# Full-width taps in one five-bank PSUM tile, a fixed split with GpSimd, and summed transforms on TensorE

## The chip, the cores and the metric

The kernel runs on one core of a Trainium2 chip. The metric is the device time of one execution in microseconds (us); lower is better. The kernel before takes 3369.24 us (median of three runs, 3368.65 to 3371.1).

## The reference

Three stages follow each other on `x` of 4 batches, 4224 tokens and 192 features.

```
w   = softmax(weight_gen over its 7 taps)         # per token and head, 8 heads of 24 features
y1[s] = sum over k of w[s, head, k] * x[s - 6 + k]  # a causal convolution of 7 taps, weights of its own per token
u   = y1 + real(fft over tokens (fft over features (y1)))
u   = u + relu(layernorm(u) @ w_ch1) @ w_ch2
th  = u @ w_theta
v   = u + w_tok_r @ (u cos th) + w_tok_i @ (u sin th)   # two 4224 x 4224 matrices over tokens
out = v + relu(v @ w_ch)
```

The change lies in the first line of work, the convolution, and in the Fourier transform that follows it.

## The kernel before, in words

The function `prologue` does the convolution and the transform. Tokens stand as 33 columns of 128 (one per partition), and a batch is cut into eight chunks of these columns: the first has five columns, the other seven have four (`SEQ`). With four batches there are 32 chunks, g = 0 to 31. A chunk of four columns and 192 features has 768 elements per partition.

For each chunk the seven taps are divided. GpSimd (`pool_taps`) multiplies the first three taps (four in the last chunk of a batch, `NPOOL`) and adds them up in a tile `pa`. VectorE (`dve_taps`) does the others: each tap is a multiplication and an addition, on two halves of 96 features. The products lie in PSUM tiles `t` of half width, three of them in rotation (`ps_t`); the running sum lies in SBUF (`xn`, named `acc` in the code). One multiplication has its weights from PSUM: ScalarE copies them into one of two PSUM tiles `wbank` (`dve_weights`, L159), always for the chunk after the next one to be computed, so that the copy for chunk g+1 is issued as chunk g begins. At the end the partial sum `pa` is added, the chunk is stored to DRAM (`xs`), and the next chunk begins.

The weights of two chunks are made by one `softmax` on 448 (or 504) elements: maximum, difference, exponential on ScalarE, sum, `1e-9` added, reciprocal, product. Its steps are set between the taps of every even chunk (`SOFT` tells after which).

The transform is a list of small steps in a queue. `rotated(d)` takes two finished chunks: TensorE turns them (L211, L223, L225), multiplies by the feature transform (L237 to L242), and ScalarE copies each result out of PSUM. `spectrum(b)` follows when a batch is complete. It has 14 groups of features: `first` (L274, then a ScalarE copy `A`, L276) and, for each pair of groups, `second` (eight matmuls L282 to L285 into two sums U and V), a ScalarE copy of U (L287), and `join`, four VectorE instructions that form U+V and U-V into `mxt`. One step of the queue is issued after every second piece of a chunk's taps (`step(1)`), eight in a chunk. All three of `first`, `second` and the turns share three PSUM buffers (`ps_f`).

Each engine works through its own instructions strictly in the order in which this code issues them. So a ScalarE copy for the transform that waits for TensorE holds back whatever ScalarE was given later: the exponential of the next softmax, or the copy of the next weights. Weights for the later stages are converted in between as well (`state["weights"]`).

When the last chunk is stored, the last batch's transform is finished beside the first steps of `main_phase`; then the large matmuls over tokens (L893) run to the end.

Of the kernel before, what the change touches and what calls it, by code (L numbers as in the profile page):

```python
# [10 lines left out]
F32 = mybir.dt.float32  # L11
# [5 lines left out]
AF = mybir.ActivationFunctionType  # L17
# [6 lines left out]
P = 128  # L24
# [2 lines left out]

SEQ = ((0, 5), (29, 4), (5, 4), (25, 4), (9, 4), (21, 4), (13, 4), (17, 4))
XO = [sum(n + 6 for _, n in SEQ[:c]) for c in range(9)]
SOFT = (1, 2, 4, 5, 7, 8)  # L30
NPOOL = (3, 3, 3, 3, 3, 3, 3, 4)
TCH = 352
NCH = S // TCH
HCH = NCH // 2
# [18 lines left out]
C2 = 0.0019353071795864769  # L53
PIC = 3.1415925
NWTS = 2 * DFF + 9 * D
NCONST = 588 + 256 + 256 + 3 * 119


def run_all(gen):
# [4 lines left out]
def prologue(tc, I, xs, mx, state):  # L64
# [12 lines left out]
    wp = pool(actx, "pw", 2)  # L77
    gp = pool(actx, "pg", 2)

    ps_w = pool(actx, "psw", 1, space=PSUM)  # L80
    wbank = [ps_w.tile([P, 512], F32, name=f"wbank{i}") for i in range(2)]
    ps_t = pool(actx, "pst", 3, space=PSUM)

    const = cp.tile([P, NCONST], F32, name="const")
    MD = const[:, 0:588].rearrange("p (s c) -> p s c", s=3)
    CS = const[:, 588:844]
    DI = const[:, 844:1100]
    BD = [const[:119, 1100 + 119 * i : 1219 + 119 * i] for i in range(3)]

    xin, wn, xn, taps, wpss = {}, {}, {}, {}, {}  # L90
    queue = state["queue"] = collections.deque()

    def load_x(g):
# [16 lines left out]
    def softmax(d):  # L110
        w, n = wn[d]
        w = w[:, :n]
        m = wbank[1][:, 5 * H * K : 5 * H * K + n]
        wide = m.unsqueeze(2).to_broadcast([P, n, K])
        nc.vector.tensor_reduce(out=m, in_=w, axis=AX.X, op=ALU.max)
        yield
        nc.vector.tensor_tensor(out=w, in0=w, in1=wide, op=ALU.subtract)
        nc.scalar.activation(w, w, AF.Exp)
        yield
        nc.vector.tensor_reduce(out=m, in_=w, axis=AX.X, op=ALU.add)  # L120
        yield
        nc.vector.tensor_scalar(m, m, 1e-9, None, op0=ALU.add)
        yield
        nc.vector.reciprocal(m, m)
        yield
# [16 lines left out]

    def pool_taps(g):
        b, c, n, d, jl = place(g)
        nt = NPOOL[c]
# [8 lines left out]
        taps[g] = (nt, pa)  # L154

    def dve_weights(g):
        b, c, n, d, jl = place(g)
        wps = wbank[g % 2][:, : 5 * H * K].rearrange("p (q k) -> p q k", k=K)
        nc.scalar.copy(wps[:, : n * H], wn[d][0][:, jl * H : (jl + n) * H])  # L159
        return wps  # L160

    def dve_taps(g):
        b, c, n, d, jl = place(g)
        nt, pa = taps.pop(g)
# [4 lines left out]
        halves = [(slice(4 * i, 4 * i + 4), slice(96 * i, 96 * i + 96)) for i in range(2)]  # L169
        ts = [None, None]  # L170
        for k in range(nt, K):
            for i, (hs, _) in enumerate(halves):
                if k == nt:
                    o = hv(xn[d], jl, n, hs)
                else:
                    ts[i] = ps_t.tile([P, 5, 96], F32, tag="tmp", name=f"t{g}{k}{i}")
                    o = hv(ts[i], 0, n, None)
                nc.vector.tensor_tensor(out=o, in0=hv(xin[g], k, n, hs), in1=wv(wps, 0, n, k, hs), op=ALU.mult)
                yield
            if k == K - 1:  # L180
                for i, (_, fs) in enumerate(halves):
                    t = ts[i][:, :n]
                    nc.vector.tensor_tensor(out=t, in0=t, in1=pa[:, :n, fs], op=ALU.add)
                    yield
            if k > nt:
                for i, (_, fs) in enumerate(halves):
                    nc.vector.tensor_tensor(out=acc[:, :, fs], in0=ts[i][:, :n], in1=acc[:, :, fs], op=ALU.add)  # L187
                    yield
        j0 = SEQ[c][0]
        nc.sync.dma_start(out=xs[b // 2][j0 : j0 + n, :, b % 2, :].rearrange("j p d -> p j d"), in_=acc)  # L190

    PQ, MX = {}, {}

# [57 lines left out]
    def spectrum(b):  # L251

        mxt = state["mxt"] = f1.tile([P, NF, D], F32, tag="mxt", name=f"mxt{b}")
        done = []

        def join(gg, ps, u):
            for i in range(2):
                V = ps[:, i, 1].rearrange("p (k e) -> p k e", e=7)
                c = 14 * gg + 7 * i
                n = 6 if c == 91 else 7  # L260
                nc.vector.tensor_tensor(
                    out=mxt[:, :, 95 + c : 95 + c + n], in0=u[:, i, :, :n], in1=V[:, :, :n], op=ALU.add
                )
                n = 5 if c == 91 else 7
                nc.vector.tensor_tensor(
                    out=mxt[:, :, c : c + n], in0=u[:, i, :, :n], in1=V[:, :, :n], op=ALU.subtract
                )

        A = {}

        def first(g):
            ps = ps_f.tile([P, 512], F32, tag="f", name=f"ps1{b}{g}")
            for c in range(2):
                nc.tensor.matmul(ps[:119, c * 256 : c * 256 + 256], PQ[b][:, c, g], CS, start=True, stop=True)  # L274
            a = A[g] = f3.tile([P, 4, P], F32, tag="A", name=f"A{b}{g}")
            nc.scalar.copy(a[:119].rearrange("p s k -> p (s k)"), ps[:119])  # L276

        def second(gg):
# [12 lines left out]
        yield  # L291
        first(1)
        yield
        for gg in range(7):
            if gg < 6:
                first(2 * gg + 2)
                yield
            r = second(gg)
            if gg < 6:
                first(2 * gg + 3)  # L300
            yield
            join(*r)
# [19 lines left out]
    for g in range(8 * B):  # L322
        if g + 2 < 8 * B:
            load_x(g + 2)
        if g % 2 and g // 2 + 2 < 4 * B:
            load_w(g // 2 + 2)
        soft = softmax(g // 2 + 1) if g % 2 == 0 and g // 2 + 1 < 4 * B else iter(())
        if g % 2 and g + 1 < 8 * B:
            pool_taps(g + 1)
        if g + 1 < 8 * B:  # L330
            wpss[g + 1] = dve_weights(g + 1)
        for n, _ in enumerate(dve_taps(g)):
            if n in SOFT:
                next(soft, None)
            if g >= 6 and n % 8 == 3:
                next(state["weights"], None)
            if n % 2:
                step(1)
        if g % 2 == 0 and g + 1 < 8 * B:
            pool_taps(g + 1)  # L340
        if g % 2:
            queue.append(rotated(g // 2))
        if g % 8 == 7:
            queue.append(spectrum(g // 8))
    actx.close()
    state["fft"] = fctx
    state["step"] = step
# [584 lines left out]
def constants():  # L932
# [11 lines left out]
    be = 2 * np.pi * ((8 * np.outer(j, j)) % NJ) / NJ  # L944
    e7 = np.eye(7)
    pad = np.zeros((P - 119, 119))
    bd = [np.concatenate([np.kron(v, e7), pad]) for v in (np.cos(be), np.sin(be), -np.sin(be))]
# [68 lines left out]
```

## Time and profile before

| | |
|---|---|
| runs, median (range) | 3369.24 us (3368.65 to 3371.1) |
| span of the profiled execution | 3368.4 us |
| TensorE matmuls | busy 3227.4 us, 96% |
| VectorE | busy 2376.5 us, 71% |
| ScalarE | busy 2096.9 us, 62% |
| GpSimd | busy 717.7 us, 21% |
| mean granted TensorE clock | 0.984 |

The page gives no other time for the profiled execution than its span, 0.8 us under the median of the runs. A span of 3368 us cut into 40 slices makes slices of 84 us; the prologue fills the first four of them. Shares over the whole span say little on it, so the rows further down are nearly all from the first 325 us.

### The profile page before, as it was taken

What the parts mean: (1) busy time and instruction counts of PE and PEld (TensorE: products, weight loads), DVE (VectorE), ACT (ScalarE), POOL (GpSimd) and SP (SyncE); (2) the same over time, 40 slices, a digit from 0 to 9 for tenths busy, and PEclk for the clock granted to TensorE, in tenths of its full rate; (3) what the DMA queues carried; (4) which work ended last, traced back from release to release, by engine and by line L of the source; (5) the groups of instructions that cost most, each with busy time, mean ns of one, the idle gap of its engine ahead of it and who ended that gap; (6) DMA issues with size and microseconds to landing.
All of it is one profiled execution on the core that took longest, in us unless ns stands there. A gap on an engine that the chain in (4) does not pass through costs nothing.

```text
span 3368.4 us, 54351 instructions
## 1 busy us (share of the span) xinstructions
PE 3227.4 (96%) x20980; PEld 3181.8 (94%) x20980; DVE 2376.5 (71%) x5338; ACT 2096.9 (62%) x3230; POOL 717.7 (21%) x662
## 2 busy tenths in 40 slices
PE   4778789999999999999999999999999999999999
PEld 3667689999999999999999999999999999999999
DVE  8998466676666666666666666676666766667666
ACT  1343456666666666666666666666666666666743
POOL 8987111111111111111111111111111111111133
PEclk8889899999999999999999999999999999999999
DMA  5554123333333333333333333333333333333333
GB/s 192 191 183 147 66 78 106 113 111 106 113 105 113 103 110 113 107 111 112 105 113 109 109 113 107 111 108 110 110 103 113 113 105 113 107 111 113 114 122 120
DMA packets 120243, 388.02 MB, mean 115 GB/s; under 512 B 10160, under 2 KB 64048, under 8 KB 119472
## 3 DMA queue, kind: packets, MB, share of 16 engines
q1 hardware_dynamic: 119696, 383.75, 33.3%
q8 instruction: 164, 2.69, 0.3%
q14 instruction: 95, 0.78, 0.1%
q10 hardware_dynamic: 288, 0.81, 0.1%
HBM read 351.88 MB, written 32.64 MB: 114 GB/s over the span
## 4 chain that ended last, share of the span: by engine, by line
PE 85%; ACT 2%; DVE 1%; POOL 0%; issue 0%; DMA 0%; ACTq 0%; POOLq 0%; DVEq 0%
PE y L893 66%; PE ch L620 4%; PE fy L832 2%; PE ch L621 2%; PE psh L598 1%; PE psh L594 1%; PE psh L597 1%; PE psh L595 1%; PE psh L596 1%; PE pst L684 1%; PE pst L672 1%; PE psu L570 1%; PE psx L650 0%; ACT cq L371 0%; ACT cq L372 0%; DVE f L380 0%
## 5 line engine op out<-in xcount | busy, mean ns | idle before, releaser
L893 PE MATMUL y<-ws,z 128*128 128x352 f32 x14256 | 2470.4, 324 | 8.4 <-DVE acc L490 3.5
L893 PEld LDWEIGHTS y<-ws,z 128*128 128x128 f32 x14256 | 2267.1, 188 | 11.4 <-DVE acc L490 4.6
L488 DVE TENSOR_TENSOR acc<-y,acc 128x352 f32<-128x352 f32 (+1 forms) x1158 | 597.2, 516 | 111.1 <-PE y L893 111.0
L387 ACT CAST ws<-f 128x704 fp32r<-128x704 f32 x396 | 309.7, 782 | 389.1 <-DVE f L380 343.3
L374 DVE SCALAR_TENSOR_TENSOR cq<-cx,cq 128x176 int32<-128x176 int32 x396 | 135.8, 343 | 470.0 <-ACT cq L372 469.6
L371 ACT ACTIVATE cq<-cq,bounds 128x704 uint8<-128x704 uint8 x396 | 348.4, 880 | 162.5 <-DVE cq L368 156.1
L726 POOL TENSOR_TENSOR r<-r,x 128x256 f32<-128x256 f32 (+1 forms) x264 | 191.8, 759 | 1156.8 <-ACT r L719 1156.8
L389 DVE TENSOR_TENSOR ws<-f,ws 128x704 fp32r<-128x704 f32 x396 | 358.0, 904 | 57.9 <-ACT ws L387 57.9
L378 ACT ACTIVATE f<-cq 128x704 int32<-128x704 int8 x396 | 312.8, 790 | 138.1 <-DVE cq L374 138.0
L380 DVE SCALAR_TENSOR_TENSOR f<-raw,f 128x704 int32<-128x704 int32 x396 | 355.9, 899 | 32.2 <-ACT f L378 31.9
L372 ACT ACTIVATE cq<-cq,bounds 128x704 uint8<-128x704 uint8 x396 | 349.3, 882 | 12.9
L366 ACT COPY cx<-raw 128x704 uint8<-128x704 uint8 x396 | 327.3, 826 | 3.1 <-DMA raw<-in_W 3.1
L607 DVE SCALAR_TENSOR_TENSOR g<-psh,g 128x256 fp32r<-128x256 f32 x384 | 162.2, 422 | 209.6 <-ACT g L606 209.6
L553 POOL TENSOR_SCALAR rs<-mv 128x2 f32<-128x2 f32 x66 | 12.6, 192 | 1185.6 <-DVE mv L552 1185.6
L620 PE MATMUL ch<-w2s,g 128*128 128x384 f32 x768 | 241.2, 350 | 1.9 <-ACT g L606 1.9
L621 PE MATMUL ch<-w2s,g 128*128 128x192 f32 x768 | 193.7, 252 | 0.1
L737 POOL TENSOR_TENSOR z<-r,z 128x768 fp32r<-128x768 f32 x66 | 122.0, 1848 | 135.6 <-ACT z L732 135.6
L621 PEld LDWEIGHTS ch<-w2s,g 128*128 128x128 f32 x768 | 145.9, 190 | 2.2 <-DVE g L607 2.0
L606 ACT ACTIVATE g<-psh 128x256 fp32r<-128x256 f32 x384 | 142.7, 372 | 8.1 <-PE ch L621 6.5
L620 PEld LDWEIGHTS ch<-w2s,g 128*128 128x128 f32 x768 | 144.6, 188 | 3.0 <-ACT g L606 2.7
L211 PE MATMUL psT<-const,xn 128*128 128x128 f32 x264 | 47.3, 339 | 92.9 <-DVE xn L187 81.1
L211 PEld LDWEIGHTS psT<-const,xn 128*128 128x128 f32 x264 | 41.8, 242 | 97.6 <-issue 54.6
(159 smaller groups left out, 3896.3 us busy)
## 6 DMA issues: line engine op xcount, KB each, us to landing
raw<-in_W SPq DMA_DIRECT2D x396, 703.6 KB
xin<-in_xa SPq DMA_DIRECT2D x28, 960.0 KB
out<-fo SPq DMA_DIRECT2D x24, 528.0 KB
mx<-mxd SPq DMA_DIRECT2D x65, 192.0 KB
xs<-xn SPq DMA_DIRECT2D x28, 384.0 KB
mxd<-mxt SPq DMA_DIRECT2D x4, 1632.0 KB
xin<-in_xa SPq DMA_DIRECT2D x4, 1056.0 KB
w<-in_wg SPq DMA_DIRECT2D x12, 224.0 KB
```

Of the source, the lines that this page charges most:

```text
L366: nc.scalar.copy(x.bitcast(U8), tops)
L371: nc.scalar.activation(q8, q8, AF.Relu, bias=bounds[:, 0:1], scale=-1.0)
L372: nc.scalar.activation(q8, q8, AF.Relu, bias=bounds[:, 1:2], scale=-8.0)
L378: nc.scalar.activation(ti, q.bitcast(I8), AF.Copy, scale=2.0**24)
L380: nc.vector.scalar_tensor_tensor(ti, words, 5, ti, op0=ALU.logical_shift_right, op1=ALU.bitwise_or)
L387: nc.scalar.copy(h, t)
L389: (eng or nc.vector).tensor_tensor(out=l(), in0=t, in1=h.bitcast(F32), op=ALU.subtract)
L488: nc.vector.tensor_tensor(out=d, in0=v, in1=d, op=ALU.add)
L620: nc.tensor.matmul(ch[:, i, 0 : 2 * D], g[:, 0, t], w, start=ft == 0, stop=False)
L621: nc.tensor.matmul(ch[:, i, D : 2 * D], g[:, 1, t], w[:, :D], start=False, stop=ft == 5)
L726: nc.gpsimd.tensor_tensor(out=o[:, ri], in0=o[:, ri], in1=x[:, :, d], op=ALU.mult)
L893: nc.tensor.matmul(ps[:, 0], zz[hl], s[:, hw, ri], start=q + n == 0, stop=q == parts_n - 1 and n == 2)
```

## The change

Four things are altered in `prologue`, and a table of constants grows by three blocks.

1. The two `wbank` tiles and the three `t` tiles are replaced by one PSUM tile `banks` of five banks (2560 elements per partition). It holds two full-width product areas `prod`, two weight areas `wts`, and the softmax's small row `m`. A tap is now one multiplication and one addition on all 192 features. A chunk's final addition (with its store) is put off until the next chunk's first multiplication has been issued (`ends`).
2. GpSimd takes three taps of every chunk, VectorE four.
3. In the softmax, `1e-9` is added by ScalarE; its steps come after the pieces 0 to 5 of a chunk, which now has eight.
4. For the first three batches TensorE forms both sums of the spectrum itself: `direct` runs eight matmuls of 238 columns for a pair of groups where `second` ran eight of 119, and `place_both` copies both results to `mxt` by ScalarE. `join` and the copy of U are left to the last batch.

```diff
-SOFT = (1, 2, 4, 5, 7, 8)
-NPOOL = (3, 3, 3, 3, 3, 3, 3, 4)
+SOFT = (0, 1, 2, 3, 4, 5)
+NPOOL = 3
...
-    wbank = [ps_w.tile([P, 512], F32, name=f"wbank{i}") for i in range(2)]
-    ps_t = pool(actx, "pst", 3, space=PSUM)
+    TW, WW = 5 * D, 5 * H * K
+    banks = pool(actx, "pst", 1, space=PSUM).tile([P, 2560], F32, name="banks")
+    prod = [banks[:, i * TW : (i + 1) * TW].rearrange("p (j d) -> p j d", d=D) for i in range(2)]
+    wts = [banks[:, 2 * TW + i * WW : 2 * TW + (i + 1) * WW] for i in range(2)]
+    mbase = 2 * (TW + WW)
...
-        nc.vector.tensor_scalar(m, m, 1e-9, None, op0=ALU.add)
+        nc.scalar.activation(m, m, AF.Identity, bias=eps[:, 0:1])
...
-        wps = wbank[g % 2][:, : 5 * H * K].rearrange("p (q k) -> p q k", k=K)
+        wps = wts[g % 2].rearrange("p (q k) -> p q k", k=K)
...
-        for k in range(nt, K):
-            for i, (hs, _) in enumerate(halves):
...
+        mult(sums, 3)
+        yield
+        if ends:
+            ends.pop()()
+            yield
+        mult(hv(prod[0], 0, n, None), 4)
+        yield
+        mult(hv(prod[1], 0, n, None), 5)
+        yield
+        add(acc, t0, acc)
+        yield
+        mult(hv(prod[0], 0, n, None), 6)
+        yield
+        add(acc, t1, acc)
+        yield
+        add(t0, t0, taps.pop(g)[:, :n])
+        yield
...
+        def direct(gg):
+            ps = ps_f.tile([P, 2, 2, 119], F32, tag="f", name=f"ps2{b}{gg}")
+            for i in range(2):
+                a = A.pop(2 * gg + i)[:119]
+                for q, (s, w) in enumerate(BOTH):
+                    nc.tensor.matmul(
+                        ps[:, i].rearrange("p s c -> p (s c)"), a[:, s], w, start=q == 0, stop=q == len(BOTH) - 1
+                    )
+            return gg, ps, None
...
-            r = second(gg)
+            r = (direct if b < 3 else second)(gg)
...
-            join(*r)
+            (place_both if b < 3 else join)(*r)
...
-            if n % 2:
-                step(1)
+            step(1)
```

On VectorE, chunk 7 (an odd one, without softmax) begins like this before. `t` are the half-width products, `wbank` the weights in PSUM, `pa` GpSimd's partial sum.

```order
L178 TENSOR_TENSOR xn_481<-xin_442,wbank_118 128x4x96 [waits DMAHW1_49]
L178 TENSOR_TENSOR xn_481<-xin_442,wbank_118 128x4x96
L178 TENSOR_TENSOR t_584<-xin_442,wbank_118 128x384
L178 TENSOR_TENSOR t_586<-xin_442,wbank_118 128x384 [waits DVE_49]
L187 TENSOR_TENSOR xn_481<-t_584,xn_481 128x4x96 [waits DVE_49]
L187 TENSOR_TENSOR xn_481<-t_586,xn_481 128x4x96 [waits DVE_49]
L178 TENSOR_TENSOR t_590<-xin_442,wbank_118 128x384
L178 TENSOR_TENSOR t_592<-xin_442,wbank_118 128x384 [waits DVE_49]
```

The two halves alternate, so a wait of VectorE on itself names an instruction two or more places ahead. Now the same chunk, whole:

```order
L180 TENSOR_TENSOR banks<-banks,pa_372 128x768 [waits DVE_49,Pool_49]
L177 TENSOR_TENSOR xn_393<-xin_368,banks 128x768 [waits DMAHW0_49,Activation_49]
L180 TENSOR_TENSOR xn_393<-banks,xn_393 128x768
L177 TENSOR_TENSOR banks<-xin_368,banks 128x768 [waits DVE_49] x2
L180 TENSOR_TENSOR xn_393<-banks,xn_393 128x768 [waits DVE_49]
L177 TENSOR_TENSOR banks<-xin_368,banks 128x768 [waits DVE_49]
L180 TENSOR_TENSOR xn_393<-banks,xn_393 128x768 [waits DVE_49]
L180 TENSOR_TENSOR banks<-banks,pa_456 128x768 [waits DVE_49,Pool_49]
```

The first row ends chunk 6. The first multiplication of chunk 7 now waits for ScalarE as well; by the values in the built program it waits for the weight copy of chunk 8. Six of the seven instructions behind it wait for VectorE, each for the instruction directly ahead of it.

On ScalarE, in the middle of the first spectrum, before: A are the copies behind `first`, U those behind `second`, L159 copies the weights of chunk 11, and L118 is the exponential of chunk 10's softmax.

```order
L276 COPY A_769<-ps_766 119x512 [waits PE_49]
L276 COPY A_785<-ps_782 119x512 [waits PE_49]
L287 COPY U_798<-ps_789 128x238 [waits DVE_49,PE_49]
L276 COPY A_803<-ps_800 119x512 [waits PE_49,Activation_49]
L159 COPY wbank_118<-w_571 128x224 [waits DVE_49]
L276 COPY A_822<-ps_819 119x512 [waits PE_49,Activation_49]
L118 ACTIVATE w_705<-w_705 128x448 [waits DMAHW6_49,DVE_49,Pool_49]
```

Now, at the same copy (L165 for the weights, L312 for `place_both`, L128 for the `1e-9`):

```order
L295 COPY A_630<-ps_627 119x512 [waits PE_49]
L312 COPY mxt_551<-ps_618 128x17x14 x2
L295 COPY A_640<-ps_637 119x512 [waits PE_49,Activation_49]
L295 COPY A_655<-ps_652 119x512 [waits PE_49,Activation_49]
L165 COPY banks<-w_466 128x224 [waits DVE_49]
L312 COPY mxt_551<-ps_643 128x17x14 x2
L124 ACTIVATE w_573<-w_573 128x448 [waits DMAHW5_49,DVE_49,Pool_49]
L413 ACTIVATE fw_669<-cqw_497 128x512
L295 COPY A_674<-ps_671 119x512 [waits PE_49,Activation_49]
L295 COPY A_690<-ps_687 119x512 [waits PE_49,Activation_49]
L128 ACTIVATE banks<-banks,eps 128x64 [waits DVE_49,Activation_49]
```

The weight copy stands behind the same copy A of the eighth `first`, in both. What it waits for has moved: by the wait's value, before it is the last multiplication of chunk 9 that reads its own `wbank`; now it is the very last addition of chunk 9, the instruction directly ahead of chunk 10's first multiplication on VectorE.

## Rows read from the trace of the kernel before

**Rows 1.** Windows: busy us of each engine, then granted TensorE clock, DMA share, GB/s.

```profile
280.00:320.00 40.00, 30.77 (x214) 28.06 (x212) 40.00 (x94) 15.42 (x39) 35.87 (x22) 0.91 0.49 165
```

**Rows 2.** Timeline at the last chunk's end: start us, us, engine, line, instruction, [idle before].

```profile
323.25 1.00 DVE L187 TENSOR_TENSOR xn<-t,xn 128x384 f32<-128x384 f32 x2
...
324.40 2.05 PE L211 MATMUL psT<-const,xn 128*128 128x128 f32 x8 [4.25 <-DVE nhalf L463]
```

**Rows 3.** Timeline of the DMA queue: the stores of chunks 7 and 23.

```profile
83.45 0.38 SPq L190 DMA_DIRECT2D xs<-xn  x1
...
245.83 0.38 SPq L190 DMA_DIRECT2D xs<-xn  x1
```

**Rows 4.** Groups by form, VectorE, 0 to 320 us: busy us, mean ns | idle before.

```profile
L178 DVE TENSOR_TENSOR t<-xin,wbank 128x384 f32<-128x384 f32 x158 | 80.9, 549 | 0.0
...
L178 DVE TENSOR_TENSOR t<-xin,wbank 128x480 f32<-128x480 f32 x24 | 15.0, 653 | 0.0
L261 DVE TENSOR_TENSOR mxt<-U,ps 128x119 f32<-128x119 f32 x39 | 10.5, 268 | 2.7 <-ACT U L287 2.7
```

**Rows 5.** VectorE timeline: the starts of chunks 3, 4 and 5.

```profile
40.40 1.01 DVE L178 TENSOR_TENSOR xn<-xin,wbank 128x384 f32<-128x384 f32 x2
...
47.83 1.01 DVE L178 TENSOR_TENSOR xn<-xin,wbank 128x384 f32<-128x384 f32 x2
...
57.97 1.01 DVE L178 TENSOR_TENSOR xn<-xin,wbank 128x384 f32<-128x384 f32 x2
```

**Rows 6.** VectorE timeline: the first softmax, where each instruction waits for the one ahead.

```profile
5.45 0.69 DVE L115 TENSOR_REDUCE wbank<-w 128x72 f32<-128x504 f32 x1 [4.57 <-DMA w<-in_wg]
6.17 0.68 DVE L117 TENSOR_TENSOR w<-w,wbank 128x504 f32<-128x504 f32 x1
7.54 0.69 DVE L120 TENSOR_REDUCE wbank<-w 128x72 f32<-128x504 f32 x1 [0.69 <-ACT w L118]
...
10.32 1.22 DVE L178 TENSOR_TENSOR xn<-xin,wbank 128x480 f32<-128x480 f32 x2 [0.46 <-ACT wbank L159]
```

**Rows 7.** Groups by form, ScalarE, 0 to 320 us.

```profile
L276 ACT COPY A<-ps 119x512 f32<-119x512 f32 x42 | 24.2, 585 | 15.3 <-PE ps L274 15.2
...
L159 ACT COPY wbank<-w 128x224 f32<-128x224 f32 x28 | 10.0, 356 | 50.0 <-DVE t L178 50.0
L287 ACT COPY U<-ps 128x238 f32<-128x238 f32 x21 | 7.5, 355 | 17.8 <-PE ps L285 14.9 <-DVE mxt L265 1.6 <-ACT w1s L387 1.0
...
L230 ACT COPY st<-psS 128x128 f32<-128x128 f32 x4 | 1.0, 261 | 0.0
```

**Rows 8.** TensorE timeline: a batch's last turn and its spectrum; two records make one matmul.

```profile
83.57 2.04 PE L211 MATMUL psT<-const,xn 128*128 128x128 f32 x8 [6.39 <-DVE xn L187]
...
92.64 2.85 PE L274 MATMUL ps<-const,PQ 128*119 128x256 f32 x12 [0.65 <-ACT PQ L245]
...
95.54 0.39 PE L283 MATMUL ps<-const,A 119*128 119x119 f32 x2
95.77 0.39 PE L284 MATMUL ps<-const,A 119*128 119x119 f32 x2
...
97.11 1.89 PE L274 MATMUL ps<-const,PQ 128*119 128x256 f32 x8
98.87 0.48 PE L282 MATMUL ps<-const,A 119*128 119x119 f32 x2
...
120.21 1.06 PE L211 MATMUL psT<-const,xn 128*128 128x128 f32 x8
```

**Rows 9.** Windows as in rows 1: that turn, and that spectrum.

```profile
83.60:88.20 4.60, 4.60 (x28) 3.88 (x28) 4.60 (x9) 1.95 (x4) 4.52 (x3) 0.59 0.84 276
92.60:120.20 27.60, 25.49 (x168) 22.47 (x169) 27.18 (x68) 13.66 (x28) 24.72 (x16) 1.00 0.40 131
```

**Rows 10.** GpSimd timeline: the starts of chunks 2 and 3.

```profile
28.32 1.54 POOL L149 TENSOR_TENSOR pa<-xin,w 128x768 f32<-128x768 f32 x1
...
36.61 1.54 POOL L149 TENSOR_TENSOR pa<-xin,w 128x768 f32<-128x768 f32 x1
```

More of the change, by code (lines that the diff above doesn't have):

```diff
@@ L55 @@
 NWTS = 2 * DFF + 9 * D
-NCONST = 588 + 256 + 256 + 3 * 119
+NCONST = 588 + 256 + 256 + 6 * 119
 def run_all(gen):
@@ L87, in prologue @@
     DI = const[:, 844:1100]
-    BD = [const[:119, 1100 + 119 * i : 1219 + 119 * i] for i in range(3)]
-    xin, wn, xn, taps, wpss = {}, {}, {}, {}, {}
+    bd = lambda i, n: const[:119, 1100 + 119 * i : 1100 + 119 * (i + n)]
+    BD = [bd(0, 1), bd(3, 1), bd(4, 1)]
+    BOTH = ((0, bd(0, 2)), (1, bd(4, 2)), (3, bd(1, 2)), (2, bd(3, 2)))
+    eps = cp.tile([P, 1], F32, name="eps")
+    nc.vector.memset(eps, 1e-9)
+    xin, wn, xn, taps, wpss, ends = {}, {}, {}, {}, {}, []
     queue = state["queue"] = collections.deque()
@@ L112, in softmax @@
         w = w[:, :n]
-        m = wbank[1][:, 5 * H * K : 5 * H * K + n]
+        m = banks[:, mbase : mbase + n]
         wide = m.unsqueeze(2).to_broadcast([P, n, K])
@@ L144, in pool_taps @@
         b, c, n, d, jl = place(g)
-        nt = NPOOL[c]
+        nt = NPOOL
         pa = gp.tile([P, 5, D], F32, tag="pa", name=f"pa{g}")
@@ L153, in pool_taps @@
                 nc.gpsimd.tensor_tensor(out=pa[:, :n], in0=pa[:, :n], in1=t[:, :n], op=ALU.add)
-        taps[g] = (nt, pa)
+        taps[g] = pa
     def dve_weights(g):
         b, c, n, d, jl = place(g)
-        wps = wbank[g % 2][:, : 5 * H * K].rearrange("p (q k) -> p q k", k=K)
+        wps = wts[g % 2].rearrange("p (q k) -> p q k", k=K)
         nc.scalar.copy(wps[:, : n * H], wn[d][0][:, jl * H : (jl + n) * H])
@@ L163, in dve_taps @@
         b, c, n, d, jl = place(g)
-        nt, pa = taps.pop(g)
         wps = wpss.pop(g)
@@ L168, in dve_taps, with mult, add, end @@
         acc = xn[d][:, jl : jl + n]
-        halves = [(slice(4 * i, 4 * i + 4), slice(96 * i, 96 * i + 96)) for i in range(2)]
-        ts = [None, None]
-        for k in range(nt, K):
-            for i, (hs, _) in enumerate(halves):
[L173 to L190, printed above, removed]
+        sums, (t0, t1) = hv(xn[d], jl, n, None), (t[:, :n] for t in prod)
+        def mult(o, k):
+            nc.vector.tensor_tensor(out=o, in0=hv(xin[g], k, n, None), in1=wv(wps, 0, n, k), op=ALU.mult)
+        def add(o, x, y):
+            nc.vector.tensor_tensor(out=o, in0=x, in1=y, op=ALU.add)
+        mult(sums, 3)
[15 more added lines that the diff above has]
+        yield
+        def end():
+            add(acc, t0, acc)
+            j0 = SEQ[c][0]
+            nc.sync.dma_start(out=xs[b // 2][j0 : j0 + n, :, b % 2, :].rearrange("j p d -> p j d"), in_=acc)
+            if g % 2:
+                queue.append(rotated(d))
+            if c == 7:
+                queue.append(spectrum(b))
+        ends.append(end)
     PQ, MX = {}, {}
@@ L276, in first, with place_both @@
             nc.scalar.copy(a[:119].rearrange("p s k -> p (s k)"), ps[:119])
+        def direct(gg):
[7 more added lines that the diff above has]
+            return gg, ps, None
+        def place_both(gg, ps, _):
+            for s, o in enumerate((95, 0)):
+                v = ps[:, :, s].rearrange("p i (k e) -> p k i e", e=7)
+                m = mxt[:, :, o + 14 * gg : o + 14 * gg + (14, 14 - s - 1)[gg == 6]]
+                if gg < 6:
+                    nc.scalar.copy(m.rearrange("p k (i e) -> p k i e", e=7), v)
+                else:
+                    nc.scalar.copy(m[:, :, :7], v[:, :, 0])
+                    nc.scalar.copy(m[:, :, 7:], v[:, :, 1, : 6 - s])
         def second(gg):
@@ L334, in prologue @@
                 next(soft, None)
-            if g >= 6 and n % 8 == 3:
+            if g >= 6 and n % 4 == 1:
                 next(state["weights"], None)
-            if n % 2:
-                step(1)
+            step(1)
         if g % 2 == 0 and g + 1 < 8 * B:
             pool_taps(g + 1)
[L341 to L344, printed above, removed]
+    ends.pop()()
     actx.close()
@@ L946, in constants @@
     pad = np.zeros((P - 119, 119))
-    bd = [np.concatenate([np.kron(v, e7), pad]) for v in (np.cos(be), np.sin(be), -np.sin(be))]
+    cb, sb = np.cos(be), np.sin(be)
+    bd = [np.concatenate([np.kron(v, e7), pad]) for v in (cb, cb, -cb, sb, -sb, -sb)]
     i2 = np.concatenate([np.eye(P), np.eye(P)], 1)
```

1 line of the change is left out of this document (removed).

## The prediction

> **What bounds the kernel now.** I read the page first. TensorE is busy 96% of the span, so the main phase will not move by itself, and the change touches nothing of it; VectorE's first slices of the page are the only full ones. The windows then show the stretch that the change does touch: from 280 to 320 us VectorE is busy 40.00 of 40 us, GpSimd 35.87, TensorE 30.77 and ScalarE 15.42 [rows 1]. The timeline at the stretch's end shows that it matters: the last addition of the last chunk ends at 324.25, and TensorE starts the last turn at 324.40, after an idle time that VectorE ended [rows 2]. All that follows hangs on that turn. So I take one microsecond of the taps' end to be one microsecond of the kernel, and the question is when the 32 chunks end. Before, chunk 7 is stored at 83.45 and chunk 23 at 245.83 [rows 3], 81.2 us for a batch.
>
> **Part 1, the full width.** A half of 384 elements takes 549 ns, of 480 elements 653 ns [rows 4], so an element costs 1.08 ns and a tap of 768 would take 0.965 us. These are lengths, not steps. Chunk 3 has 16 halves and no softmax, and lasts from 40.40 to 47.83 [rows 5]: 0.464 a step, 0.085 less than the length, because VectorE starts an instruction before the one ahead has ended. It does so when it need not wait for that one. In the first softmax it must: L115 starts at 5.45, lasts 0.69, and L117 starts at 6.17 [rows 6], 0.03 behind the end. So a full-width instruction steps by 0.88 when free and by 0.995 when held by its predecessor, against 0.93 for the two halves it replaces. Holding costs 0.115 and turns a gain of 0.05 into a loss of 0.065.
>
> The changed order decides which it is. Before, the two halves alternate, so each wait names an instruction two or more places ahead. Now six of eight instructions in an odd chunk wait for the one directly ahead. Only some of these are true needs: the multiplication of tap 5 does not use what tap 4's wrote. But products, weights and the softmax row are parts of one tile, and the waits are set as if any access to the tile touched any other. In an even chunk nine are held, softmax included.
>
> On the cost of such a wait the Trainium skill speaks against my reading: "VectorE: DVE Perf Modes", section "The DRAIN you can't avoid", says that the pipe empties after every instruction anyway and that a semaphore between two of them costs nothing extra, and the rules of that page advise fewer instructions, not fewer semaphores. By that rule the merged taps would gain; it is one of the rivals below. The trace does not bear it out: the step is shorter than the length by 0.085 where nothing holds [rows 4, 5] and longer by 0.03 where the predecessor does [rows 6].
>
> **Part 2, the weight copy as a fence.** The same coarse tile ties the first multiplication of chunk g to ScalarE's copy for chunk g+1, and that copy to the last addition of chunk g-1. So at each chunk's start VectorE stops, ScalarE copies, VectorE goes on. A copy takes 356 ns [rows 7]; the one start of this kind in the trace shows 0.46 idle for a copy somewhat larger [rows 6]. I take 0.40, and the 0.085 of lost overlap: 0.485 a chunk. In even chunks the `1e-9`, now ScalarE's, does the same between two VectorE instructions. No row has it; between nothing and the 0.585 of ScalarE's longest copy here I take its shortest, 0.26 [rows 7], two hand-overs of 0.03, and the lost overlap: 0.405.
>
> An odd chunk is then 8 x 0.88 + 6 x 0.115 + 0.485 = 8.2 us (7.43 before). An even chunk lasted 57.97 - 47.83 = 10.14 [rows 5], 2.71 more than an odd one; about 0.1 of it leaves with the `1e-9`. Now: 7.04 + 2.6 + 9 x 0.115 + 0.405 + 0.485 = 11.6. A batch is four of each and 1.7 for its five-column chunk: 80.8. The same count before gives 4 x 7.43 + 4 x 10.14, 1.6 more for the five columns and 1.9 less for the tap that GpSimd took: 70.0. `join` adds 28 x 0.18 = 5.1 [rows 4]. The rest of the 81.2, 6.1, is weight conversion and small waits.
>
> **Part 3, GpSimd.** A chunk of three taps takes it 36.61 - 28.32 = 8.29 [rows 10], about 68 a batch. That is below VectorE's 80.8: it will wait, and the tap taken from it buys nothing.
>
> **Part 4, TensorE's sums, and who waits for them.** A matmul of 119 columns steps by 95.77 - 95.54 = 0.23, one of 256 by (98.87 - 97.11)/4 = 0.44 [rows 8], at a granted clock of 1.00 [rows 9], the 2.4 GHz level. For 238 columns I interpolate 0.41. `first` is two of 256, 0.88. A pair of groups was 8 x 0.23 + 2 x 0.88 = 3.6 and becomes 8 x 0.41 + 1.76 = 5.04. Seven pairs: 10 us more TensorE per batch. Before, the spectrum from 92.64 to 120.21 [rows 8] fitted behind VectorE's 81. The fence takes that slack away, because the weight copy stands in ScalarE's queue behind copies that wait for TensorE. Set t = 0 at the start of chunk 8, the first behind a complete batch. Its first multiplication (five columns, held, 1.2), the softmax's maximum (0.65) and the deferred addition (0.965) end at about 2.85; the turn takes 92.64 - 83.57 = 9.07 [rows 8], partly at a granted clock of 0.59 [rows 9] since TensorE had idled before it; the spectrum starts at 11.9.
> - Chunk 9's first multiplication is behind two `first` and their copies (0.28 + 0.585) and the weight copy: 11.9 + 1.76 + 0.87 + 0.42 = 14.95. VectorE alone would be there at 13.1: 1.9 lost.
> - Chunk 10's is behind eight `first` and three `direct`: 11.9 + 7.0 + 9.8 + 0.87 + 0.42 = 30. VectorE alone, 8.4 and a conversion after 14.95: 23.8. Lost 6.2.
> - Chunk 11's is behind five more `first` and two `direct`, 12.6 us at most with ScalarE held by the softmax; chunk 10 itself lasts as long. Lost about nothing.
> - Chunk 12's is behind the spectrum's last pairs and three copies of the next turn, at 52.9; VectorE alone at 50.9. Lost 2.
>
> That is 10.1 a batch, three times. The conversions that fall into these stalls no longer count, half of the 6.1. A batch with a spectrum: 80.8 + 10.1 + 3 = 94 (81.2 before). ScalarE's new copies of 238 elements, as long as the copy of U, 355 ns [rows 7], are two where one was, and hide behind TensorE. In the first batch there is no spectrum, but the same fence waits for the turns: 9.07 against the 8.7 that an even chunk has left behind the deferred addition, and a longer turn in chunk 2; I put 2.5 for that batch.
>
> **Sum.** Chunk 0's taps start at 10.3 [rows 6]. Chunk 8 starts at 10.3 + 80.8 + 2.5 = 93.6, chunk 24 at 93.6 + 2 x 94 = 281.6. The last eight lack one softmax (3.4): 90.6, and the deferred addition 1.0: 373.2. Before: 324.25. The taps end 49 us later. The span 3368.4 becomes 3417.4, and with the 0.8 us by which the runs' median lies above it, 3418.
>
> **Rivals.**
> - *The waits cost nothing and the widths count* (faster). For it: fewer instructions, and `join` gone. Against it: rows 6. Price: taps 58.0 a batch against 59.2, so -5 over four; sixteen `1e-9`, -2; three times `join`, -15. The taps end at 302, GpSimd at about 285 does not stop that: 3347. It decides if the fence stays below 0.2 a chunk and the held steps at 0.88.
> - *Held, but ScalarE is never late.* For it: ScalarE is busy only 15.42 of 40 us [rows 1]. Against it: its copies `A` and U idle for TensorE at its queue's head, 15.3 and 14.9 us [rows 7], and whatever stands behind them idles too. 10.3 + 80.8 + 2 x 86.9 + 83.5 + 1 = 349.4: 25 later, 3394.
> - *TensorE at its lower level in the spectrum.* It now waits for VectorE's stops and ran at 0.59 in a turn behind an idle stretch [rows 9]. If half of the 23 us of `direct` ran at half the clock, 11.5 a batch: 3452. Against it: in the spectrum it still has work most of the time.
> - *The taps' end is hidden*, some load or conversion being late anyway: 3369. Rows 2 speak against it.
>
> **Numbers.** Forecast 3418, chance 0.62, its own range 3400 to 3436. ScalarE never late 0.16, lower clock 0.12, waits free 0.06, hidden 0.04. The range 3380 to 3450 leaves out the last two and half of the lower clock, 0.16. Its low end also makes room for fences of 0.2 instead of 0.485, 9 us over 32 chunks. A change under 0.2% (7 us) can't be told from none: faster 0.06, same 0.04, slower 0.90.
>
> **What would show it.** VectorE's timeline in an odd chunk without spectrum: about 8.2 between the first multiplications, steps near 1.0, and a gap of 0.4 ahead of each chunk that ends with ScalarE's weight copy. In chunks 8 to 12, 16 to 20 and 24 to 28: a gap of several us at chunk 10, 18, 26, ended by that copy behind an `A`. GpSimd idle for VectorE in most chunks. The last turn starts near 373. Steps of 0.88 would prove part 1 wrong; chunk 10 starting without a gap, part 4.

## The result, and the profile after

The changed kernel takes 3413.88 us (median of four runs, 3413.68 to 3415.57), beside 3368.94 us for the kernel before on the same chip: a ratio of 1.0135, 95% interval 1.0121 to 1.0148, so it is slower. The profiled execution has a span of 3412.2 us at a mean granted TensorE clock of 0.98.

The first view to read is the end of the prologue, the answer to [rows 2]: timeline of the kernel after, start, duration, engine, line, instruction, and in brackets the idle time before it.

```profile
366.95 0.96 DVE L180 TENSOR_TENSOR xn<-banks,xn 128x768 f32<-128x768 f32 x1
...
368.05 2.05 PE L230 MATMUL psT<-const,xn 128*128 128x128 f32 x8 [5.91 <-DVE nhalf L498]
```

The taps end at 367.91 (366.95 + 0.96) where they ended at 324.25: 43.7 us later, and the span is 43.8 us longer. So the loss lies in the prologue. The windows show how it is spread. Each row is one stretch: busy time of TensorE, its weight loads, VectorE, ScalarE and GpSimd, then the granted clock. After, from chunk 8's start to chunk 16's, then the last turn ahead of the spectrum in it, then the spectrum:

```profile
93.56:186.25 92.69, 71.32 (x400) 62.87 (x400) 76.98 (x90) 34.76 (x88) 68.36 (x42) 0.87 0.47 163
93.56:105.38 11.82, 8.22 (x48) 7.30 (x48) 10.95 (x14) 4.09 (x10) 9.57 (x6) 0.71 0.31 104
105.38:141.55 36.17, 35.45 (x169) 31.09 (x169) 26.41 (x30) 14.90 (x35) 22.36 (x14) 1.00 0.39 139
```

And before, from chunk 8's start to chunk 16's:

```profile
83.34:164.09 80.75, 61.88 (x400) 54.59 (x400) 80.33 (x184) 32.36 (x75) 75.64 (x45) 0.90 0.55 184
```

VectorE has 3.35 us less to do in such a batch (76.98 against 80.33), and the batch is 11.9 us longer. Before, VectorE was idle for 0.4 us of it; now for 15.7. The change took work from the engine that sets the end and made it wait.

Where it waits, a chunk without softmax and without spectrum shows first. VectorE's timeline after, chunk 3 and the start of chunk 4, which answers to the first two starts of [rows 5]:

```profile
44.52 0.95 DVE L177 TENSOR_TENSOR xn<-xin,banks 128x768 f32<-128x768 f32 x1 [0.55 <-ACT banks L165]
45.39 0.95 DVE L180 TENSOR_TENSOR xn<-banks,xn 128x768 f32<-128x768 f32 x1
46.38 1.96 DVE L177 TENSOR_TENSOR banks<-xin,banks 128x768 f32<-128x768 f32 x2
48.37 0.96 DVE L180 TENSOR_TENSOR xn<-banks,xn 128x768 f32<-128x768 f32 x1
49.36 0.96 DVE L177 TENSOR_TENSOR banks<-xin,banks 128x768 f32<-128x768 f32 x1
50.36 0.96 DVE L180 TENSOR_TENSOR xn<-banks,xn 128x768 f32<-128x768 f32 x1
51.42 0.97 DVE L180 TENSOR_TENSOR banks<-banks,pa 128x768 f32<-128x768 f32 x1
52.85 0.95 DVE L177 TENSOR_TENSOR xn<-xin,banks 128x768 f32<-128x768 f32 x1 [0.47 <-ACT banks L165]
```

Most steps are 0.99 to 1.0, longer than the instruction itself (0.96); the addition of `pa`, which also waits for GpSimd, comes 1.06 behind its predecessor, and the second row, which is not held, 0.87. The bracket at each chunk's start is the fence: VectorE stands still while ScalarE copies the next chunk's weights. The chunk lasts 8.33 us (7.43 before).

In a batch with a spectrum the same bracket grows. The starts of chunks 8 to 12:

```profile
93.56 1.15 DVE L177 TENSOR_TENSOR xn<-xin,banks 128x960 f32<-128x960 f32 x1 [0.47 <-ACT banks L165]
108.28 0.95 DVE L177 TENSOR_TENSOR xn<-xin,banks 128x768 f32<-128x768 f32 x1 [1.76 <-ACT banks L165]
123.35 0.95 DVE L177 TENSOR_TENSOR xn<-xin,banks 128x768 f32<-128x768 f32 x1 [6.34 <-ACT banks L165]
135.79 0.95 DVE L177 TENSOR_TENSOR xn<-xin,banks 128x768 f32<-128x768 f32 x1 [0.41 <-ACT banks L165]
144.57 0.95 DVE L177 TENSOR_TENSOR xn<-xin,banks 128x768 f32<-128x768 f32 x1 [0.92 <-ACT banks L165]
```

The releaser named is the weight copy, a thing of 0.35 us. What it stood behind is on ScalarE's timeline just before chunk 10 starts:

```profile
107.89 0.35 ACT L165 COPY banks<-w 128x224 f32<-128x224 f32 x1
...
118.37 0.62 ACT L295 COPY A<-ps 119x512 f32<-119x512 f32 x1
122.48 0.59 ACT L295 COPY A<-ps 119x512 f32<-119x512 f32 x1 [3.49 <-PE ps L293]
122.96 0.35 ACT L165 COPY banks<-w 128x224 f32<-128x224 f32 x1
```

ScalarE is idle for 3.49 us at the head of its queue, for a copy `A` that waits for TensorE, and the weight copy that VectorE waits for is behind it. That copy, at 122.96, brings the weights of chunk 11. The weights of chunk 10 itself were copied at 107.89, some 15 us before its first multiplication: what it waits for is a neighbour in its tile, not something that it uses. TensorE meanwhile works at the period that its timeline shows, 5.04 us for a pair of groups (113.02 to 118.06):

```profile
113.02 3.47 PE L302 MATMUL ps<-const,A 119*128 119x238 f32 x16
116.33 1.89 PE L293 MATMUL ps<-const,PQ 128*119 128x256 f32 x8
118.06 3.47 PE L302 MATMUL ps<-const,A 119*128 119x238 f32 x16
```

The waits of the first 365 us, grouped (engine, line, releaser: total us, times, longest), name the same chain:

```profile
POOL pa L155 <- DVE banks L180: 67.7, 19, 10.0
ACT A L295 <- PE ps L293: 48.6, 21, 3.5
DVE xn L177 <- ACT banks L165: 34.6, 31, 6.3
...
DVE xn L180 <- ACT banks L128: 5.8, 14, 0.4
```

The copies `A` waited 15.2 us before [rows 7]; now 48.6. GpSimd, with three taps everywhere, waits 67.7 us for VectorE (17.9 in the kernel before).

### The profile page after: what moved, and what is told of

It is laid out like the page before. It is cut to its first block, busy times and chain, and to the rows that moved or that the text cites. A ratio compares the mean times of both kernels' runs of the same rounds, so it can differ in the third digit from the quotient of the medians.

```text
span 3412.2 us, 54100 instructions
## 1 busy us (share of the span) xinstructions
PE 3252.8 (95%) x20980; PEld 3204.0 (94%) x20980; DVE 2376.2 (70%) x4999; ACT 2106.7 (62%) x3273; POOL 704.5 (21%) x654
## 4 chain that ended last, share of the span: by engine, by line
PE 83%; ACT 2%; DVE 1%; POOL 0%; issue 0%; DMA 0%; ACTq 0%; POOLq 0%; DVEq 0%
PE y L928 65%; PE ch L655 4%; PE fy L867 2%; PE ch L656 2%; PE psh L629 1%; PE psh L633 1%; PE psh L632 1%; PE psh L630 1%; PE psh L631 1%; PE pst L719 1%; PE pst L707 1%; PE psu L605 1%; PE psx L685 0%; ACT cq L406 0%; ACT cq L407 0%; DVE f L415 0%
```

## The experiments

In the table, "batch" runs from chunk 8's start to chunk 16's, with the busy time of VectorE and TensorE in it; "taps end" is the end of the last chunk's last addition. Ratios are to the kernel before, run on the same chip. "Sums" are the spectrum's two sums formed by TensorE, "paced" is six steps of the transform in a chunk instead of eight, and "tiles apart" takes the five-bank tile to pieces; the edits stand below.

| kernel | median us | ratio (95%) | batch | VectorE | TensorE | taps end |
|---|---|---|---|---|---|---|
| before | 3368.9 | | 80.75 | 80.33 | 61.88 | 324.25 |
| after | 3413.9 | 1.0135 (1.0121–1.0148) | 92.69 | 76.98 | 71.32 | 367.91 |
| old second, join | 3409.5 | 1.0126 (1.0111–1.0141) | 90.78 | 81.04 | 63.54 | 363.05 |
| weights apart | 3409.9 | 1.0128 (1.0112–1.0145) | 91.81 | 76.25 | 72.03 | 364.08 |
| tiles apart | 3395.3 | 1.0085 (1.0070–1.0100) | 88.02 | 73.03 | 71.09 | 350.47 |
| after, paced | 3392.4 | 1.0073 (1.0058–1.0088) | 85.50 | 76.47 | 71.55 | 348.01 |
| apart, paced | 3365.6 | 0.9991 (0.9981–1.0000) | 80.18 | 73.04 | 71.12 | 319.58 |
| apart, paced, join | 3366.8 | 0.9996 (0.9987–1.0006) | 80.72 | 78.89 | 64.19 | 322.45 |
| before with sums | 3380.0 | 1.0037 (1.0024–1.0050) | 83.47 | 74.73 | 69.78 | 335.99 |
| same, paced | 3362.0 | 0.9985 (0.9975–0.9994) | 78.53 | 75.17 | 70.93 | 316.70 |
| before, paced | 3364.9 | 0.9990 (0.9981–0.9999) | 79.64 | 79.64 | 65.34 | 321.04 |
| pair copy, 4th tap | 3363.9 | 0.9988 (0.9979–0.9997) | 82.90 | 76.09 | 69.42 | 320.39 |
| pair copy, two 4th taps | 3372.1 | 1.0012 (1.0003–1.0020) | 83.98 | 72.96 | 70.81 | 326.10 |
| pair copy | 3361.7 | 0.9979 (0.9969–0.9988) | 80.90 | 74.70 | 70.42 | 316.68 |

In all fourteen the span is 3041 to 3045 us longer than "taps end". So, to within those 4 us, one microsecond there is one of the kernel, as the prediction took it.

**Old second and join in the changed kernel.**

```diff
-            r = (direct if b < 3 else second)(gg)
+            r = (direct if b < 0 else second)(gg)
...
-            (place_both if b < 3 else join)(*r)
+            (place_both if b < 0 else join)(*r)
```

> The changed kernel with its old second and join for all four batches (before 3368.9, after 3413.9). Theory: the held steps and the weight copy as a fence stay, so an odd chunk without a spectrum lasts 8.2 to 8.5 us and the gap ahead of each chunk stays near 0.4. The join's 5.1 us a batch come back on VectorE, and the stalls at chunks 9 and 10 of a batch shrink by some 6 us, since a pair of groups takes TensorE 3.6 us and not 5.0. A batch with a spectrum 91 to 94 us (92.65 after), the whole 3405 to 3419: about the same as after. Rival, TensorE's doubled matmuls are the loss: the 25 us that the stalls of chunks 9 and 10 cost over three batches go and the kernel comes to about 3388.

The result is 3409.5, as the theory had it. The stall at chunk 10 falls from 6.34 to 1.23 us, but VectorE's busy time rises by 4.1 us, and only 1.9 us of the batch are left as gain. The rival falls.

**Weights in a tile of their own.**

```diff
-    banks = pool(actx, "pst", 1, space=PSUM).tile([P, 2560], F32, name="banks")
+    banks = pool(actx, "pst", 1, space=PSUM).tile([P, 2048], F32, name="banks")
...
+    wbank = pool(actx, "psw", 1, space=PSUM).tile([P, 512], F32, name="wbank")
+    wts = [wbank[:, :WW], wbank[:, WW : WW + 4 * H * K]]
```

Both weight areas lie in this one new tile; in the kernel before each had a tile of its own.

> The changed kernel with the weights in a PSUM tile of their own (products and the softmax row stay together in a tile of four banks). Theory: the weight copy then waits only for the last multiplication that read its half, two additions before the chunk's end, so the fence's gap of 0.4 to 0.5 us goes at some 24 chunk starts where no spectrum holds ScalarE up; the held steps, the gap at the 1e-9 and the stalls at chunk 10 of a batch stay. 8 to 13 us less than after: 3401 to 3406, and VectorE's idle time that ends with the weight copy falls from 32 to about 22 us or less. Rival, only held steps count and the fence is hidden: 3414, unchanged.

The kernel takes 3409.9, 4.0 us less than after and not 8 to 13, and VectorE's idle time on that copy hardly falls:

```profile
DVE xn L178 <- ACT wbank L166: 33.2, 15, 6.9
```

31 waits have become 15, of nearly the same sum. The first batch, where no spectrum stands in the queue, is 2.8 us shorter (11.54 to 90.70, against 11.64 to 93.56). Only one side of the fence is gone. The copy for chunk g+1 no longer waits for the last addition of chunk g-1, but the first multiplication of chunk g still waits for that copy, which writes the other half of `wbank`. Where ScalarE is late, VectorE reaches this wait earlier and waits longer (6.93 at chunk 10), so the batch from chunk 8 is only 0.9 us shorter: most of what the first side cost there is now waited for at the second.

**Products apart, and apart from the weights.** The two products get tiles of two banks each, the softmax's row the end of the second; the weights are as in the run before, two areas in one tile.

```diff
-    prod = [banks[:, i * TW : (i + 1) * TW].rearrange("p (j d) -> p j d", d=D) for i in range(2)]
...
+    pt = [pst.tile([P, 1024], F32, name=f"prod{i}") for i in range(2)]
+    prod = [t[:, :TW].rearrange("p (j d) -> p j d", d=D) for t in pt]
```

> The changed kernel with its two products in two PSUM tiles of two banks and the weights in a third, so that a multiplication into one product no longer waits for the addition that reads the other. Theory: free steps of 0.88 us in place of 0.99 for three to five instructions of a chunk, and the fence gone; chunk 10 of a batch still waits for TensorE through ScalarE's queue and starts about 30 us after chunk 8, which hides a part of the gain there. A batch with a spectrum 86 to 88 us, the whole 3385 to 3395. Rival, waits between instructions of VectorE cost nothing (the Trainium skill's rule): only the fence's part of the gain comes, 3401 to 3406 as with the weights alone in a tile of their own.

The kernel takes 3395.3, 18.6 less than after and just above the theory's range. VectorE's timeline in chunk 3 has the reason, row by row against the one above:

```profile
41.85 0.95 DVE L178 TENSOR_TENSOR xn<-xin,wbank 128x768 f32<-128x768 f32 x1 [2.38 <-ACT wbank L166]
42.72 0.95 DVE L181 TENSOR_TENSOR xn<-prod,xn 128x768 f32<-128x768 f32 x1
43.70 1.83 DVE L178 TENSOR_TENSOR prod<-xin,wbank 128x768 f32<-128x768 f32 x2
45.44 0.95 DVE L181 TENSOR_TENSOR xn<-prod,xn 128x768 f32<-128x768 f32 x1
46.43 0.96 DVE L178 TENSOR_TENSOR prod<-xin,wbank 128x768 f32<-128x768 f32 x1
47.30 0.95 DVE L181 TENSOR_TENSOR xn<-prod,xn 128x768 f32<-128x768 f32 x1
48.16 0.96 DVE L181 TENSOR_TENSOR prod<-prod,pa 128x768 f32<-128x768 f32 x1
49.03 0.95 DVE L178 TENSOR_TENSOR xn<-xin,wbank 128x768 f32<-128x768 f32 x1
```

The same eight instructions, of the same lengths, take 7.18 us in place of 8.33. Steps that nothing holds are 0.87; those that a true need holds (the addition at 42.72 and the multiplication behind it share product 0) are still 0.98 to 0.99. Four steps became shorter by 0.12 to 0.20, and the stop of 0.47 behind the last addition is gone. The rival, that such waits cost nothing, falls. The bracket of 2.38 shows what is left: the first multiplication of chunk 3 still waits for the copy of chunk 4's weights, here late behind the turn's copies.

**The changed kernel, six steps a chunk.**

```diff
-            step(1)
+            if n < 6:
+                step(1)
```

> The changed kernel with six steps of the transform in a chunk (after its first six pieces) instead of eight. Theory: what holds VectorE at chunks 9, 10 and 12 of a batch is the weight copy behind copies that wait for TensorE, so with fewer of them in a chunk those stalls (1.8, 6.3 and 0.9 us in after) fall to the fence's 0.4 to 0.5, while the conversions that they hid come back. VectorE alone needs 82.9 us a batch in after's own chunk lengths (four of 8.33, four of 11.97, 1.7 for the five columns) and 4 to 6 of conversion: 87 to 89 instead of 92.65, the whole 3397 to 3403. Rival, TensorE's 10 us more a batch are the limit whatever the pace: 3410 to 3418.

The kernel takes 3392.4, 21.5 less than after, with the same instructions on every engine in another order. The starts of chunks 8 to 12:

```profile
93.31 1.15 DVE L177 TENSOR_TENSOR xn<-xin,banks 128x960 f32<-128x960 f32 x1 [0.47 <-ACT banks L165]
106.69 0.95 DVE L177 TENSOR_TENSOR xn<-xin,banks 128x768 f32<-128x768 f32 x1 [0.42 <-ACT banks L165]
115.29 0.95 DVE L177 TENSOR_TENSOR xn<-xin,banks 128x768 f32<-128x768 f32 x1 [0.42 <-ACT banks L165]
127.73 0.95 DVE L177 TENSOR_TENSOR xn<-xin,banks 128x768 f32<-128x768 f32 x1 [0.41 <-ACT banks L165]
136.01 0.95 DVE L177 TENSOR_TENSOR xn<-xin,banks 128x768 f32<-128x768 f32 x1 [0.42 <-ACT banks L165]
```

Every stall in these chunks is back at the bare fence, and chunk 12 starts 42.7 us behind chunk 8 instead of 51.0. A smaller stall comes up later, 1.51 at chunk 14 where after has 0.41. The gain was some 5 to 11 us larger than the theory's; its rival, TensorE's time as such, falls: TensorE is as busy (71.55) in a batch 7.2 us shorter.

**Apart and paced, with TensorE's sums and without.** The two edits above together; the second kernel has the old `second` and `join` as well.

> Products and weights in tiles of their own and six steps of the transform in a chunk. Theory: both losses go. VectorE alone needs 69.3 us a batch at the chunk lengths of the run with the tiles apart (four of 7.18, four of 9.72, 1.7 for the five columns), 4 to 6 of conversion and a few small waits: 75 to 80 instead of 88.4, with GpSimd close behind at 68; the whole 3348 to 3368, below the kernel before. Rival, TensorE's time sets the batch whatever the pace: 3385 to 3396, as with the tiles apart alone.

> Tiles apart and six steps in a chunk as in the run beside it, but with the old second and join in all batches. Theory: VectorE is again what sets the batch, and join's 5.1 us a batch come back on it: 12 to 16 us more than with the sums on TensorE, 3362 to 3380. Rival, TensorE sets the batch there: 3 x 10 us less for it, so less than the run beside it.

They take 3365.6 and 3366.8, both inside their theories' ranges: together the two edits take 48.3 us off after, though they took 18.6 and 21.5 one by one. Which of the two kernels is faster can't be told. The windows of their batches say why:

```profile
84.18:164.36 80.18, 71.12 (x400) 63.52 (x400) 73.04 (x91) 34.19 (x88) 71.32 (x44) 0.90 0.55 187
```

```profile
84.71:165.43 80.72, 64.19 (x400) 55.92 (x400) 78.89 (x119) 32.80 (x79) 69.79 (x43) 0.88 0.54 186
```

With the sums on TensorE (first row) VectorE is busy 5.9 us less and idle 5.3 us more. The expectation for the second kernel, 12 to 16 us more, was wrong: it held VectorE's work for the bound of both.

**TensorE's sums alone in the kernel before, then paced, then the pace without the sums.** `direct` and `place_both` as in the change; for the pace:

```diff
-            if n % 2:
+            if n in (1, 3, 5, 7, 9, 11):
                 step(1)
```

> The kernel before with TensorE's sums alone, at its old pace of eight steps a chunk. Theory: join's 5.1 us leave each of three batches, but the exponential of the softmax and the weight copies now stand behind copies that wait for TensorE, some 9 us a batch: 3375 to 3381. Rival, before has no fence and so nothing is late: 3354, 15 us less.

> The kernel before with one part of the change alone, the sums formed by TensorE for three batches (join gone there), and with six steps of the transform in a chunk instead of eight, so that TensorE is not asked for more in a chunk than it can do and ScalarE's queue does not hold copies that wait for it. Theory: 28 x 0.18 = 5.1 us of join less in each of three batches, and at most a third of it lost again to waits: 3355 to 3362. Rival, what is lost by direct is TensorE's time as such (10 us a batch), whatever the pace: no gain, 3369 or more.

> The kernel before with six steps of the transform in a chunk instead of eight and nothing else: second and join stay. It tells whether the 6 us that the kernel before gained with TensorE's sums and six steps came from the sums or from the pace. Theory: VectorE hardly waits in the kernel before, so the pace alone gives nothing, 3365 to 3371, and the sums are worth 4 to 8 us once they are paced. Rival, it was the pace: 3360 to 3364.

At the old pace the sums cost 12 us (3380.0, as the theory had it), with no five-bank tile in the kernel. The timeline shows the chain at chunk 10, this time through the `wbank` tile that holds the softmax's row and the weights of the odd chunks:

```profile
105.27 1.00 DVE L180 TENSOR_TENSOR xn<-xin,wbank 128x384 f32<-128x384 f32 x2
...
110.23 0.59 ACT L278 COPY A<-ps 119x512 f32<-119x512 f32 x1 [3.49 <-PE ps L276]
110.71 0.64 ACT L295 COPY mxt<-ps 128x238 f32<-128x238 f32 x2
...
111.22 0.38 ACT L161 COPY wbank<-w 128x224 f32<-128x224 f32 x1
...
111.64 0.63 DVE L117 TENSOR_REDUCE wbank<-w 128x64 f32<-128x448 f32 x1 [5.37 <-ACT wbank L161]
```

The first row starts chunk 10 without a wait, though the copy of chunk 11's weights comes only at 111.22, 6 us later. No chunk behind the first waits for that copy at its start in this kernel, whose two weight areas are two tiles. The softmax's maximum waits, because its row shares a tile with the weights being copied. So a copy that is late by less than a chunk costs VectorE nothing by itself here; in after and in this kernel it costs through a tile that holds something else as well.

Paced, the sums give 3362.0, as the theory's upper end had it, and the pace alone gives 3364.9, between its two ranges and just below no change (0.9990, 0.9981 to 0.9999). The intervals of the two overlap, so what the sums are worth once paced (2.9 us by the medians, 1.7 by the ratios) stays open. Why the pace helps the kernel before can be read from its waits: `join` waited 2.7 us for ScalarE's copies of U [rows 4], and with six steps it does not wait at all; that is most of the 3.2 us by which the taps end earlier in the two traces.

**One weight copy for two chunks.** Tiles apart and paced; the copy is issued behind the odd chunk's last multiplication. The first version gives GpSimd a fourth tap in chunk 7 of a batch, the second in chunks 3 and 7, the third nowhere (and has a third buffer for the loaded weights).

```diff
-        if g + 1 < 8 * B:
-            wpss[g + 1] = dve_weights(g + 1)
...
+            if n == 5 and g % 2 and g + 1 < 8 * B:
+                dve_weights(g // 2 + 1)
```

> Tiles apart and six steps a chunk, and two things more: one weight copy for two chunks, issued right behind the odd chunk's last multiplication, in place of one for each chunk; and GpSimd takes the fourth tap of a batch's last chunk again. Theory: of the 17 us that VectorE still waits for the weight copy with the tiles apart and paced, half leave, and a multiplication and an addition of 0.87 leave in each of four batches: 3348 to 3360. Rival, VectorE's waits only move to GpSimd (71 us a batch then) or to TensorE: 3362 to 3367, as without.

> The run beside it, with a fourth tap for GpSimd in the fourth chunk of a batch as well. VectorE has 1.74 us a batch less, GpSimd 2.8 more (about 74). Theory: VectorE still sets the batch, 3 to 7 us less than the run beside it. Rival, GpSimd is late at that chunk's end or in the first batch, where nothing else holds VectorE up: no gain.

> The run with one weight copy for two chunks, with three taps for GpSimd in every chunk and a third buffer for the softmax's weights, so that their load need not wait for GpSimd. GpSimd was busy 75.8 of a batch's 81.5 us there, which is taken as the reason why VectorE gained nothing. Theory: GpSimd falls to about 71, VectorE is at 73 to 77 a batch, the whole 3350 to 3361. Rival, TensorE through ScalarE's queue still sets the batch: 3362 to 3367 as in the other paced runs.

The first two miss what the theory hoped for. The first, 3363.9, is where its rival put it; the second, 3372.1, is 8.2 us slower than the first where its rival said no gain. In the second GpSimd is the bound: its busy time (fifth of the five) is 82.49 of a batch's 83.98, and the last addition waits for it:

```profile
82.47:166.45 83.98, 70.81 (x400) 63.23 (x400) 72.96 (x88) 34.04 (x84) 82.49 (x50) 0.90 0.57 189
```

```profile
323.97 2.13 DVE L180 TENSOR_TENSOR xn<-pa,xn 128x768 f32<-128x768 f32 x1 [4.41 <-POOL pa L159]
```

In the first GpSimd is busy 81.41 of 82.90, but what VectorE waits for longest there is still the weight copy, 10.7 us in all; that GpSimd is the bound there too is likely and not shown. With three taps it is 3361.7, at a ratio of 0.9979 (0.9969 to 0.9988): a little faster than the kernel before, and in ratio the lowest of all, though its interval overlaps those of five other kernels in the table. It lies between the theory's range and the rival's.

## Why the prediction was right, and where its sizes were off

The forecast was 3418; 3413.9 lies inside its own range, by the mechanism that it named.

*Full width.* Held steps were to be 0.995 and free ones 0.88; they are 0.99 to 1.0 and 0.87. The tiles apart show that the hold and not the width costs: same instructions, 1.15 us less a chunk, 0.56 of it at the fence. On this the Trainium skill, "VectorE: DVE Perf Modes", section "The DRAIN you can't avoid", says of eight copies in a row that a semaphore behind each costs nothing extra; it also says that an instruction which is not held starts earlier. These runs agree with the second: they put 0.12 us on each step that a wait on the predecessor holds, and where the first would have it free the measurement decides.

*The fence.* Idle 0.41 to 0.47 at most starts where 0.40 was taken; the `1e-9` copy lasts 0.288 (0.26 taken) and leaves 0.4 idle. An odd chunk was to last 8.2 and an even one 11.6; they last 8.33 and 11.9. What the forecast did not see is that the fence's price and the stalls' do not simply add: with the copy freed from the last addition, most of what was saved was waited for at the next late copy (the run with the weights apart).

*The stalls.* The working put chunk 9 at +14.95 behind chunk 8, chunk 10 at +30 and chunk 12 at +52.9; measured +14.7, +29.8 and +51.0. So the first two came almost exactly out of TensorE's rows and the interpolated 0.41 for a matmul of 238 columns (eight take 116.33 - 113.02 = 3.31). The place of chunk 12 is mis-sized: 2 us were to be lost there, and its bracket of 0.92 holds only 0.5 beyond the fence. The three brackets together hold 7.6 us beyond the fence, where 10.1 was to be lost.

*The sum.* The taps were to end at 373.2, and end at 367.9. Chunk 0 starts 1.3 late (11.64 for 10.3), since the loaded weights arrive 0.9 later, and the first softmax has the `1e-9` copy and a longer fence in it too. The start of that softmax, after, beside the 5.45 of [rows 6]:

```profile
6.33 0.69 DVE L121 TENSOR_REDUCE banks<-w 128x72 f32<-128x504 f32 x1 [5.43 <-DMA w<-in_wg]
```

The first batch is 81.9 for 83.3, the two with a full softmax 92.7 for 94, and the last 89.1 for 91.6: 1.3 - 1.4 - 2.7 - 2.5 = -5.3. That the batches came so close has some luck in it: the chunks' own lengths are 1.8 us a batch above the 80.8 of the working (four of 8.33, four of 11.9, and the 1.7), and the stalls 2.5 below the 10.1.

*GpSimd.* It has slack, as said: 68.36 busy of 92.69. Neither the fixed split nor the `1e-9` on ScalarE was taken back by itself, so what each costs the changed kernel is not shown.

*The rivals.* ScalarE never late: it is late, and pacing alone is worth 21.5 us. What makes its lateness cost anything at a chunk's start is the tile: in "before with sums" the copy at chunk 10 is 6 us late and no chunk's start waits for it. No run gives the changed kernel's two weight areas a tile each, so how much of the stalls would go by that alone stays open. TensorE at its lower level in the spectrum: its granted clock there is 1.00, the 2.4 GHz level; it is 0.71 in the turn before, behind an idle 7 us, as in [rows 9]. Waits that cost nothing, and a hidden end, are both excluded by the kernels above.

What the prediction left unsaid is that its two losses cover each other. Tiles apart and pace take 17.4 and 19.9 us off the taps' end one by one, but 48.3 together. With the tiles apart alone, VectorE gets to the late copies sooner and waits longer there (7.40 at chunk 10 for 6.34); with the pace alone, only the shorter stalls that the held steps left could go.

## What to carry to other kernels

Before fewer and wider instructions are counted as a gain, look which tile each of them shares with its neighbours: waits set by the whole tile can cost more than the merge saves, and a tile shared with another engine turns into a fence, even where the two use different parts of it. A short copy that the bounding engine waits for must not be issued behind copies that wait for a slower engine; if it must, issue fewer of those per unit of the bounding engine's work. Where the wait is only for a neighbour in a tile, a tile of its own for the copy is the first thing to try; here that was tried for the products, and not for the two weight areas. And if one removed wait gives less than it should, try it together with the next one before it is given up.

## What was not expected of the hardware

The length of a VectorE instruction did not change with its tiles: 0.95 to 0.97 us for 768 elements in the chunks shown, held or not. All of the difference lies in when the next one starts. And the same weight conversion lasts 0.28 us in one place and 1.89 in another, here in the kernel before, with the GpSimd instruction that was running when it started:

```profile
102.96 1.81 POOL L153 TENSOR_TENSOR pa<-pa,pb 128x768 f32<-128x768 f32 x1
103.03 1.89 DVE L374 SCALAR_TENSOR_TENSOR cqw<-cxw,cqw 128x128 int32<-128x128 int32 x1
...
142.96 1.54 POOL L149 TENSOR_TENSOR pb<-xin,w 128x768 f32<-128x768 f32 x1
144.41 0.28 DVE L374 SCALAR_TENSOR_TENSOR cqw<-cxw,cqw 128x128 int32<-128x128 int32 x1
```

The first ends 0.15 us behind the end of its GpSimd instruction (104.77), the second 0.19 behind its own (144.50). All 24 conversions of this kind in the prologues of four traces (before, before paced, after, and apart and paced) end 0.15 to 0.21 us behind the end of the GpSimd instruction that they started in, so their length goes with how much of it was left. No run moved one engine against the other, and what the two share is not shown.
